# Score-tile windows, fewer matmuls on zeros, and another front in a planned attention and mixer kernel

## The chip, the core and the metric

The kernel runs on one core of a Trainium2 chip. The metric is the device time of one execution in microseconds (us); the kernel before takes 1763.97 us in the median of three runs (1763.39 to 1764.01). The engines are TensorE (PE in the profile, PEld for its weight loads), VectorE (DVE), ScalarE (ACT), GpSimd (POOL) and SyncE (SP), which issues nearly all of the transfers.

## What is computed

Two layers, each an attention block and a mixer over tokens, on x of 2048 tokens by 640 features. There are 32 heads of 20 features:

```python
def _A_ref(x, wqkv, wo):
    B, S, D = x.shape
    H = 32
    Dh = D // H
    qkv = (lambda x, *d: x.transpose(*d))((x @ wqkv).reshape(B, S, 3, H, Dh), 2, 0, 3, 1, 4)
    q, k, v = qkv[0], qkv[1], qkv[2]
    scores = jnp.einsum("bhqd,bhkd->bhqk", q, k) * (Dh ** -0.5)
    p = _softmax(scores, axis=-1)
    o = jnp.einsum("bhqk,bhkd->bhqd", p, v)
    return (lambda x, *d: x.transpose(*d))(o, 0, 2, 1, 3).reshape(B, S, D) @ wo

def _B_ref(x, w1, b1, w2, b2):
    h = _layernorm(x, axis=-1)
    u = jnp.einsum("bsd,sf->bdf", h, w1) + b1
    u = _gelu(u)
    y = jnp.einsum("bdf,fs->bds", u, w2) + b2
    return (lambda x, *d: x.transpose(*d))(y, 0, 2, 1)

x = x + _A_ref(_layernorm(x, axis=-1), A_wqkv, A_wo)
x = x + _B_ref(_layernorm(x, axis=-1), B_w1, B_b1, B_w2, B_b2)
```

The last two lines run twice. In each layer 32 x 2048 x 2048 scores have to be exponentiated, which is most of the work.

## The kernel before, in words

**Tiling.** Tokens are cut into 16 tiles of 128, queries into 4 blocks of 512, and heads into 8 groups of 4. A *unit* is one query block, one head group and one tile of keys (`unit_order`, line 468): four *chunks* of 128 keys by 512 queries, one for each head of the group. A chunk's scores are one matmul on a strip of 32 rows of the array (line 700), and the four heads' strips run beside each other. They land in a PSUM bank. There are eight banks: banks 0 to 2 form the wide score tile (three chunks), banks 3 and 4 the narrow one (two chunks), bank 6 accumulates the output, and banks 5 and 7 are shared by everything else.

**Two ways to exponentiate.** ScalarE takes the wide and the narrow tile in turn and applies Exp to three or two chunks at once (`do_exp`, line 880; the activation is line 887). VectorE takes whole units of its own, one bank per chunk: it scales each chunk to a 16-bit integer tile J (`do_J`, line 840), and then forms five terms T of J whose bit patterns, read as bf16, add up to the exponential (`do_T`, line 860). Which units go to VectorE is decided in `d_take` (line 786): a unit is taken if VectorE would end it before ScalarE gets to the end of that group.

**After the exponential** TensorE multiplies by V (`do_PV`, line 927), in groups of four chunks on four column strips. V is stored as `Vaug`, 24 columns for each head: 20 of values, one of ones, whose product is the softmax denominator, and padding. At a group's end VectorE transposes the sums (line 976) and takes a reciprocal (line 988), GpSimd multiplies (line 995), and VectorE transposes back (line 1003).

**Fills.** All other matrix work is cut into *fills* (`add_fill`, line 366): the projections of Q, K and V, the output projection, and the mixer's two products. A fill accumulates in bank 5 or 7 (in any free bank where no attention runs) and is copied out by ScalarE or VectorE (`copy`, lines 461 and 463; L456 and L453 are its matmuls). `do_fill` (line 410) runs a burst of up to 400 ns of one fill, and stops it early where the next matmul would end after `s_at[0] + FILL_OVER`, the time at which the next score tile can start; FILL_OVER is 0.0.

**What sets the order.** No scheduler reorders anything: under a manual schedule, `run_until` (line 1535) keeps one planned clock for each engine, asks each engine's chooser for its next job and start, and emits the earliest one. The planned durations are constants of the file. So the order on every engine is fixed when the program is built, and on the chip each engine runs its list in order and waits for semaphores. The planner for TensorE is `pe_choose`. It collects the options: the next score tile (priority 0), a score tile for VectorE (0.9), PV groups, and a fill (1 if urgent, else 4), each with its start. It then keeps those that start within 30 ns of the earliest, and those of priority 1 or better that start within a *window* of their own; the best priority wins:

```python
opts.append((s_at[0], 0, WIN_S[a.next_slot()], a.do_SA))
...
e0 = min(o[0] for o in opts)
ok = [o for o in opts if o[0] <= e0 + 30 or (o[1] <= 1 and o[0] <= e0 + o[2])]
o = min(ok, key=lambda o: (o[1], o[0]))
```

`WIN_S` (line 72) has that window for the wide tile (slot 0) and the narrow one (slot 1), in planned ns.

**Matmuls on zeros.** The same function keeps a history of TensorE's planned work in the last 3413 ns, counted in slots of 216 ns. Where the best option is more than 250 ns away and the history holds less than `HAM_MIN` (line 82), it emits a matmul on zeros instead (`do_warm`, line 1466). Ten more stand at the very start (line 1588).

**The front.** `front` (line 1556) loads four token tiles, the weights of Q and of K (`load_w`), two more token tiles, V's weights wv, and the other token tiles, all on SP's queue, which holds eight transfers at a time. The weights are copied into padded tiles by ScalarE or VectorE (`pad_copies`). Each token tile goes through statistics on VectorE (lines 343 to 346), a scale on GpSimd (`scale_job`, lines 354 and 356), its application on VectorE (line 530), transposes on TensorE (line 541) and a copy to hh. ScalarE zeroes the padding of Q's and K's weights (line 1586), and then writes V's padding and ones (lines 1591 and 1593). GpSimd follows with two small memsets of V (lines 1594 and 1596).

Of the kernel before, what the change touches and what calls it, by code (L numbers as in the profile page):

```python
# [21 lines left out]
H = 32  # L22
# [46 lines left out]
LAT_V = 120.0  # L69
EXP_CH = 453.0  # L70
D_SLACK = 0.0
WIN_S = (160.0, 160.0)
FILL_OVER = 0.0
M_F = 0.0
SD_WAIT = 500.0
# [3 lines left out]
FILL_NS = 400.0  # L79
COL_FILL = True  # L80
URG = 16
HAM_MIN = 10.0
DMA_RATE = 400.0
DMA_LAT = 1600.0

# [41 lines left out]
def kernel(  # L127
# [135 lines left out]
    def push(eng, prio, ready, dur, fn, ok=None, table=None):  # L263
        seq[0] += 1
        jobs[eng].append((prio, ready, seq[0], dur, fn, ok, table))
# [84 lines left out]
    def scale_job(prio, ready, mv, then, double):  # L350

        def f(start):
            rt = stat.tile([128, 1], F32, name="rt")
            nc.gpsimd.tensor_scalar(out=rt[:], in0=mv[:, 1:2], scalar1=(1.0 + LN_EPS) if double else 1.0,
                                    scalar2=LN_EPS * LN_EPS if double else LN_EPS, op0=ALU.mult, op1=ALU.add)
            nc.gpsimd.tensor_tensor(out=rt[:], in0=rt[:], in1=mhalf[:], op=ALU.pow)
            nmr = None
            if double:
                nmr = stat.tile([128, 1], F32, name="nmr")
                nc.gpsimd.tensor_tensor(out=nmr[:], in0=mv[:, 0:1], in1=rt[:], op=ALU.mult)  # L360
                nc.gpsimd.tensor_scalar(out=nmr[:], in0=nmr[:], scalar1=-1.0, scalar2=None, op0=ALU.mult)
            then(rt, nmr, start + (1250 if double else 900) + 150)
        push("POOL", prio, ready, 1250 if double else 900, f)


    def add_fill(mms, cost, evac, ecost, ready=0.0, pr=5, ok=None, urgent=None, acost=None, eprio=2, bf16=None, on_start=None,
# [1034 lines left out]
    def pe_choose():  # L1401
# [46 lines left out]
        o = min(ok, key=lambda o: (o[1], o[0]))  # L1448
        while hist and hist[0][0] < now - 3413:
            hist.popleft()  # L1450
        if o[0] > now + 250 and sum(h[1] for h in hist) < HAM_MIN and now > 2000:
            if a.want and not a.done and not a.acc_open():
                return (o[0], o[3])
            if a.want and not a.done or bank_free[5] is not None and bank_free[5] <= now:
                return (now + (SW if pe_mode[0] != "col" else 0.0), do_warm)
# [100 lines left out]
    def front(L0):  # L1556
        def load_x0(tt):
            def f(sl, t):
                tl = sb("x0", [128, D], BF16, sl)
                dma(tl[:], A_x[0, tt * 128:(tt + 1) * 128, :], 128 * D * 2, t,  # L1560
                    then=lambda t: L0.token_tile(tt, tl[:], t, lambda t: rX0.give(sl, t)))
            rX0.want(f)

        def load_w(i):
            wr = sb("wraw", [128, NDT, D], BF16, i)
            coff = 0 if i else D
            dma(wr[:], A_wqkv[:, coff:coff + D].rearrange("(dt p) n -> p dt n", p=128), 128 * NDT * D * 2,
                rate=DMA_RATE * (0.5 if i else 0.9), then=lambda t: pad_copies(i, wr, t))
        for tt in range(4):
            load_x0(tt)  # L1570
        load_w(1)
        load_w(0)
        for tt in range(4, 6):
            load_x0(tt)
# [12 lines left out]
        for _ in range(N_WARM0):  # L1587
            nc.tensor.matmul(ps(6, [128, 512])[0:32, :], lhsT=zw[:, 0:32], rhs=ident[:].unsqueeze(1).to_broadcast([128, 4, 128]), start=True, stop=True, tile_position=(0, 0))

        v_pad = Vv[:, :, :, DH:VW].rearrange("p k h c -> p (k h) c")  # L1590
        nc.scalar.activation(out=v_pad.bitcast(F32), in_=mhalf[:, 0:1].unsqueeze(2).to_broadcast([128, NKT * H, (VW - DH) // 2]),
                             func=ACT.Copy, scale=0.0)
        nc.scalar.activation(out=v_pad[:, :, 0:1], in_=mhalf[:, 0:1].unsqueeze(2).to_broadcast([128, NKT * H, 1]), func=ACT.Copy, scale=-2.0)
        nc.gpsimd.memset(Vaug[:, NKT * H * VW:], 0.0)

        nc.gpsimd.memset(Vv[:, :, H // 2, 0:32 - VW], 0.0)
        clk.update(ACT=6000.0, DVE=1100.0, POOL=2200.0, PE=1300.0 + 427.0 * N_WARM0)

    def late_weights():
        nc.gpsimd.memset(wo_pad[:].rearrange("p a b -> p (a b)"), 0.0)  # L1600
# [56 lines left out]
```

## Time and profile before

| | |
|---|---|
| Median of three runs | 1763.97 us |
| The profiled execution's own time | 1763.39 us |
| Its span, first to last instruction | 1761.6 us |
| PE, DVE, ACT, POOL busy | 1673.1, 1531.1, 1589.0, 181.1 us |
| Mean granted TensorE clock | 0.992 |
| Wide exponential (128x1536), 660 | 1486 ns each |
| Narrow exponential (128x1024), 659 | 1063 ns each |
| J, 796, and T, 995, on VectorE | 677 and 703 ns each |

In the profile a line such as `L887 ACT ACTIVATE P<-pst` is a group of instructions: source line, engine, operation, and what it writes and reads. After the bar come the busy time and the mean of one, and behind the next bar how long the engine had been idle ahead of them and what ended that. Durations of one instruction overlap a little with the next, so that a stream of exponentials starts them somewhat closer together than their mean. TensorE's busy time contains the matmuls on zeros. In the windows by stage each row has a stretch's start and end and its length, then the busy time of PE, PEld, DVE, ACT and POOL with the number of instructions, then the granted clock of TensorE as a share of full speed, the share of the transfer engines, and GB/s. The first layer's exponentials run from 20 to 817 us and the second layer's from about 870 to 1683 us; between 800 and 1000 us the first mixer's last products and the second layer's projections run too, and the second mixer's last products end the kernel.

### The profile page before, as it was taken

Reading aid. Unit: us, or ns where it says so; the run is one execution under the profiler, and the core shown is the slowest. Engines: PE = TensorE matmul, PEld = TensorE weight load, DVE = VectorE, ACT = ScalarE, POOL = GpSimd, SP = SyncE. Lnnn points to the kernel's source line nnn. Section 1 sums busy time; section 2 is a strip of 40 time slices with the busy share of each in tenths; the row PEclk is TensorE's granted clock in tenths of the full one; section 3 lists DMA queues with packets and bytes.
Section 4 is the critical chain, followed back from the end, with each engine's and each line's share of the span. In section 5 each row is a group of like instructions: output and inputs, shape, how many; then the busy total and the mean of one; then the engine's idle time right before and its main releaser. Section 6 shows DMA issues by size and latency. Waiting matters only on the chain.

```text
span 1761.6 us, 50941 instructions
## 1 busy us (share of the span) xinstructions
PE 1673.1 (95%) x22105; PEld 644.4 (37%) x22105; DVE 1531.1 (87%) x2715; ACT 1589.0 (90%) x1441; POOL 181.1 (10%) x297
## 2 busy tenths in 40 slices
PE   8999999999999999998999999999999999999989
PEld 3433233222333233334545432332333333333356
DVE  6788999999989999998444699999998999989973
ACT  7799999999999999997598799999999999999940
POOL 3100012000200020002100000210012000200010
PEclk8999999999999999999999999999999999999999
DMA  3200001000222015520422000100012210365133
GB/s 117 28 2 2 2 13 35 1 2 1 62 71 63 17 40 183 164 62 21 141 71 81 32 2 2 39 24 1 1 31 70 69 59 1 122 181 174 46 96 97
DMA packets 103298, 98.10 MB, mean 56 GB/s; under 512 B 45600, under 2 KB 79520, under 8 KB 103072
## 3 DMA queue, kind: packets, MB, share of 16 engines
q1 hardware_dynamic: 99456, 94.82, 17.6%
q8 instruction: 173, 2.83, 0.7%
q0 software_dynamic: 3616, 0.01, 0.3%
q14 instruction: 53, 0.43, 0.1%
HBM read 63.35 MB, written 31.46 MB: 54 GB/s over the span
## 4 chain that ended last, share of the span: by engine, by line
PE 45%; DVE 41%; ACT 7%; issue 4%; DMA 2%; POOL 1%; SPq 0%; DVEq 0%; POOLq 0%; ACTq 0%
DVE JT L860 17%; PE pst L456 15%; DVE JT L840 14%; PE pst L700 12%; PE pst L927 12%; ACT P L887 6%; PE pst L453 5%; DVE T_85 L976 2%; DVE attnT L1003 1%; DMA W<-in_B_w_dram 1%; DVE QT L463 1%; DVE x1last L1088 1%; DVE bnst L343 1%; DVE bnst L344 1%; DVE rden L988 1%
## 5 line engine op out<-in xcount | busy, mean ns | idle before, releaser
L887 ACT ACTIVATE P<-pst 128x1024 bf16<-128x1024 f32 (+1 forms) x1321 | 1512.5, 1273 | 42.8 <-PE pst L700 26.3
L860 DVE TENSOR_SCALAR JT<-JT 128x2048 uint16<-128x2048 uint16 x995 | 669.7, 703 | 3.2
L700 PE MATMUL pst<-QT,KT 32*128 32x512 bf16 (+1 forms) x4224 | 577.0, 377 | 33.9 <-ACT P L887 20.7
L840 DVE TENSOR_SCALAR JT<-pst 128x512 uint16<-128x512 f32 x796 | 528.0, 677 | 66.9 <-PE pst L700 47.7
L927 PE MATMUL pst<-P,Vaug 128*32 128x512 bf16 (+1 forms) x3396 | 516.3, 380 | 3.1 <-DVE T_85 L976 2.2
L927 PE MATMUL pst<-JT,Vaug 128*32 128x512 bf16 (+1 forms) x4140 | 499.9, 376 | 14.7 <-DVE T_85 L976 9.1
L700 PEld LDWEIGHTS <-KT 32*128 32x128 bf16 x4224 | 155.1, 91 | 501.4 <-issue 492.5
L927 PEld LDWEIGHTS <-Vaug 128*32 128x32 bf16 x7536 | 181.9, 94 | 319.3 <-issue 284.8
L995 POOL TENSOR_TENSOR T_86<-T_85,rden 128x512 bf16<-128x512 f32 x64 | 68.2, 1065 | 1184.4 <-DVE rden L988 1144.7
L1466 PE MATMUL pst<-ident,zw 128*32 128x512 bf16 (+1 forms) x390 | 125.7, 376 | 0.0
L456 PEld LDWEIGHTS <-W 128*32 128x32 bf16 x3384 | 88.7, 96 | 63.3 <-issue 31.5
L456 PE MATMUL pst<-wo,attnT 128*32 128x320 bf16 x1984 | 105.2, 301 | 3.7 <-DVE JT L840 1.4
L456 PE MATMUL pst<-hh,wq 128*32 128x512 bf16 x1232 | 102.9, 382 | 2.3 <-DVE JT L840 1.8
L456 PE MATMUL pst<-hh,wk 128*32 128x512 bf16 x1240 | 96.9, 381 | 1.5 <-DVE hh L463 0.7
L456 PE MATMUL pst<-x1last,W 128*32 128x320 bf16 x1536 | 81.6, 301 | 0.4
L456 PEld LDWEIGHTS <-attnT 128*32 128x32 bf16 x1984 | 49.6, 95 | 48.4 <-issue 32.4
L456 PE MATMUL pst<-attnT,hh 128*32 128x320 bf16 x1196 | 58.9, 300 | 3.2 <-ACT hh L461 0.7
L456 PE MATMUL pst<-JT,W 128*32 128x320 bf16 x1080 | 52.6, 300 | 0.3 <-issue 0.3
L1003 DVE STREAM_TRANSPOSE attnT<-T_86 128x512 bf16<-128x512 bf16 (+1 forms) x66 | 44.9, 682 | 2.1 <-POOL T_86 L995 2.0
L1466 PEld LDWEIGHTS <-zw 128*32 128x32 bf16 x390 | 35.2, 96 | 31.1 <-issue 17.3
L456 PE MATMUL pst<-hh,W 128*32 128x320 bf16 x768 | 40.5, 301 | 6.0 <-DMA W<-in_B_w_dram 4.7
L456 PEld LDWEIGHTS <-wq 128*32 128x32 bf16 x1232 | 32.6, 95 | 34.4 <-issue 20.2
(94 smaller groups left out, 893.4 us busy)
## 6 DMA issues: line engine op xcount, KB each, us to landing
W<-in_B_w_dram SPq DMA_DIRECT2D x10, 768.0 KB
W<-in_B_w_dram SPq DMA_DIRECT2D x24, 256.0 KB
xs<-in_A_x_dram SPq DMA_DIRECT2D x32, 160.0 KB
x2d<-xs SPq DMA_DIRECT2D x16, 320.0 KB
xs<-x2d SPq DMA_DIRECT2D x16, 320.0 KB
x1d_69<-xs SPq DMA_DIRECT2D x12, 320.0 KB
uacca_72<-W SPq DMA_DIRECT2D x12, 320.0 KB
W<-uacca_72 SPq DMA_DIRECT2D x12, 320.0 KB
```

The costliest lines, as they stand in the source:

```text
L343: nc.vector.bn_stats(out=bst[:, 0, :], in_=src[:, 0:half])
L453: nc.tensor.matmul(out_, lhsT=lhsT, rhs=rhs, start=start, stop=stop)
L456: nc.tensor.matmul(out_[32 * c:32 * c + 32], lhsT=lhsT[:, 32 * c:32 * c + 32], rhs=rhs, start=start, stop=stop, tile_position=(0, 32 * c))
L700: pe(nc.tensor.matmul(dst, lhsT=k_, rhs=q_, start=True, stop=True, tile_position=(32 * j, 0)))
L840: nc.vector.tensor_scalar(out=c["jt"][:, j * 512:(j + 1) * 512], in0=Dt[:], scalar1=SCALE * LOG2E * 256.0, scalar2=127.0 * 256.0, op0=ALU. ...
L860: nc.vector.tensor_scalar(out=tt_[:], in0=c["jt"][:], scalar1=0.5, scalar2=TERM_C[i], op0=ALU.mult, op1=ALU.add)
L887: nc.scalar.activation(out=P[:, 0:n, :].rearrange("p a b -> p (a b)"), in_=St[:, 0:n, :].rearrange("p a b -> p (a b)"), func=ACT.Exp, scal ...
L927: pe(nc.tensor.matmul(dst, lhsT=Vaug[:, n:n + 32], rhs=ap, start=acc["cnt"][j] == 1 and not part, stop=last[j] and (half is None or part = ...
L976: nc.vector.transpose(out=T1[:], in_=src[:, 0:w])
L995: eng.tensor_tensor(out=T2[:], in0=T1v, in1=rden.unsqueeze(2).to_broadcast([128, w // 32, 32]), op=ALU.mult)
L1003: nc.vector.transpose(out=attnT[(qb, g)][:, q0:q1], in_=T2[:].rearrange("p c i -> p (c i)"))
L1466: pe(nc.tensor.matmul(dst[0:32, 0:128 * n], lhsT=zw[:, 0:32], rhs=ident[:].unsqueeze(1).to_broadcast([128, n, 128]), start=not inside, sto ...
```

## The change

The window of the wide score tile goes from 160 to 330 ns, that of the narrow one from 160 to 100. The history below which a matmul on zeros is emitted goes from 10 to 8 slots, and none is emitted in the first 12 us of the plan (before: 2). The plan's durations for GpSimd's scale become shorter (1250 to 1000, and 900 to 750 ns), and so do its estimates of when the weights have landed. In the front, two token tiles are loaded ahead of Q's weights instead of four, and two between Q's and K's. V's padding and ones are written by four memsets on GpSimd, as a job of the plan with priority 5, not before 9 us and 4.6 us long, in place of ScalarE's two writes. FILL_OVER, and the place where a burst of fills stops, are the same in both files.

```diff
-WIN_S = (160.0, 160.0)
+WIN_S = (330.0, 100.0)
 FILL_OVER = 0.0
...
-HAM_MIN = 10.0
+HAM_MIN = 8.0
...
-            then(rt, nmr, start + (1250 if double else 900) + 150)
-        push("POOL", prio, ready, 1250 if double else 900, f)
+            then(rt, nmr, start + (1000 if double else 750) + 150)
+        push("POOL", prio, ready, 1000 if double else 750, f)
...
-        if o[0] > now + 250 and sum(h[1] for h in hist) < HAM_MIN and now > 2000:
+        if o[0] > now + 250 and sum(h[1] for h in hist) < HAM_MIN and now > 12000:
...
             dma(wr[:], A_wqkv[:, coff:coff + D].rearrange("(dt p) n -> p dt n", p=128), 128 * NDT * D * 2,
-                rate=DMA_RATE * (0.5 if i else 0.9), then=lambda t: pad_copies(i, wr, t))
-        for tt in range(4):
+                then=lambda t: pad_copies(i, wr, t))
+        for tt in range(2):
             load_x0(tt)
         load_w(1)
+        for tt in range(2, 4):
+            load_x0(tt)
         load_w(0)
         for tt in range(4, 6):
             load_x0(tt)
...
-        v_pad = Vv[:, :, :, DH:VW].rearrange("p k h c -> p (k h) c")
-        nc.scalar.activation(out=v_pad.bitcast(F32), in_=mhalf[:, 0:1].unsqueeze(2).to_broadcast([128, NKT * H, (VW - DH) // 2]),
-                             func=ACT.Copy, scale=0.0)
-        nc.scalar.activation(out=v_pad[:, :, 0:1], in_=mhalf[:, 0:1].unsqueeze(2).to_broadcast([128, NKT * H, 1]), func=ACT.Copy, scale=-2.0)
-        nc.gpsimd.memset(Vaug[:, NKT * H * VW:], 0.0)
-
-        nc.gpsimd.memset(Vv[:, :, H // 2, 0:32 - VW], 0.0)
-        clk.update(ACT=6000.0, DVE=1100.0, POOL=2200.0, PE=1300.0 + 427.0 * N_WARM0)
+        def v_ones(start):
+            nc.gpsimd.memset(Vv[:, :, :, DH:VW], 0.0)
+            nc.gpsimd.memset(Vaug[:, NKT * H * VW:], 0.0)
+            nc.gpsimd.memset(Vv[:, :, :, DH:DH + 1], 1.0)
+
+            nc.gpsimd.memset(Vv[:, :, H // 2, 0:32 - VW], 0.0)
+        push("POOL", 5, 9000.0, 4600.0, v_ones)
+        clk.update(ACT=5000.0, DVE=1100.0, POOL=2200.0, PE=1300.0 + 427.0 * N_WARM0)
```

## The prediction

> **What bounds the kernel now.** I read the page's busy times first, then the chain of waits, then the busy time by stage, then who waited for whom in the long attention stretches, and last the first 20 us on each engine.
>
> ```profile
> span 1761.6 us, 50941 instructions
> PE 1673.1 (95%) x22105; PEld 644.4 (37%) x22105; DVE 1531.1 (87%) x2715; ACT 1589.0 (90%) x1441; POOL 181.1 (10%) x297
> PE 45%; DVE 41%; ACT 7%; issue 4%; DMA 2%; POOL 1%; SPq 0%; DVEq 0%; POOLq 0%; ACTq 0%
> L887 ACT ACTIVATE P<-pst 128x1024 bf16<-128x1024 f32 (+1 forms) x1321 | 1512.5, 1273 | 42.8 <-PE pst L700 26.3
> L1466 PE MATMUL pst<-ident,zw 128*32 128x512 bf16 (+1 forms) x390 | 125.7, 376 | 0.0
> ```
>
> Three engines are close to full together. The second group is not work: 390 matmuls on zeros that only keep TensorE busy. By stage (PE, PEld, DVE, ACT, POOL busy, then granted clock):
>
> ```profile
> 100.00:800.00 700.00, 669.19 (x8724) 228.46 (x8716) 662.34 (x1134) 679.93 (x597) 64.10 (x90) 1.00 0.15 45
> 800.00:1000.00 200.00, 188.73 (x3016) 101.96 (x3013) 107.98 (x221) 152.38 (x162) 21.71 (x52) 0.99 0.24 76
> 1000.00:1600.00 600.00, 580.18 (x7651) 198.71 (x7650) 567.11 (x981) 583.29 (x512) 61.27 (x87) 1.00 0.16 49
> ```
>
> In the two attention stretches ScalarE is idle for only 20.1 of 700 us and 16.7 of 600 us, VectorE for 37.7 and 32.9. The chain passes often through VectorE, since what ends last alternates, but ScalarE has the least room. Of its idle time between 100 and 1600 us, and VectorE's, the largest parts that the attention loop makes are (us, times, longest):
>
> ```profile
> ACT P L887 <- PE pst L700: 24.4, 51, 2.2
> ACT P L887 <- PE pst L927: 8.7, 14, 1.7
> DVE JT L840 <- PE pst L700: 43.5, 79, 1.3
> ```
>
> So 24.4 us is all that a better-timed score tile could give back to the exponentials there. The clock matters next:
>
> ```profile
> 338.50:341.95 3.45, 2.08 (x25) 0.73 (x18) 3.34 (x6) 2.77 (x3) 0.00 (x0) 1.00 0.00 0
> 341.95:345.35 3.40, 3.28 (x18) 1.00 (x17) 3.37 (x8) 2.37 (x2) 1.05 (x1) 0.50 0.02 5
> 345.35:348.80 3.45, 3.45 (x41) 0.96 (x39) 3.15 (x6) 3.08 (x3) 0.00 (x0) 1.00 0.00 0
> ```
>
> TensorE was busy for 2.08 of 3.45 us (60%), with waits of 0.52, 0.62 and 0.35 us; then the clock was halved for 3.4 us. It happened once in the long attention stretches. Last, the front:
>
> ```profile
> 5.26 2.55 ACT L1593 ACTIVATE Vaug<-mhalf 128x512 bf16<-128x512 f32 x1
> 7.87 0.20 POOL L1596 MEMSET Vaug<- 128x128 bf16 x1 [5.69 <-ACT Vaug L1593]
> 8.16 0.19 POOL L354 TENSOR_SCALAR rt<-mv 128x1 f32<-128x1 f32 x1
> 9.53 0.71 PE L541 MATMUL pst<-ident,attnT 128*128 128x128 bf16 x5 [4.34 <-DVE attnT L530]
> GB/s 0 213 224 191 324 372 371 364 363 364 143 20 0 11 0 20 269 38 5 11 0 0 0 0 108 2 0 11 0 0 0 50 65 70 93 69 68 71 62 154
> ```
>
> GpSimd stood 5.7 us behind ScalarE's write of V's ones before it could scale the first token tile, whose statistics were ready at 4.2 us. The last line is the load rate in steps of 1.5 us.
>
> **The change part by part.** The kernel writes its instruction order at build time, so a constant moves every instruction; I compare the two built programs by counts. The words "fill bursts stop" have no edit behind them: that stop and its allowance (0.0) are in both, and runs of filling matmuls number 828 before and 832 after.
>
> *Front, taken −1 us.* Off ScalarE go two writes (1.09 + 2.55 = 3.64 us); they held the first scale from 4.2 to 8.16 us, so 3.9 us is the most to gain. What is late next: in the new order TensorE has eight of V's projections ahead of Q's, and they need wv, the ninth load, as before. Adding up the rate line, its 3.44 MB are in at about 13.0 us. The cold 512-column rows of wq took 3.15 us for 7 before, 0.43 each with the overlap off, so 320 columns take about 0.27 and eight of them 2.2 us; so Q starts at about 15.2 against 13.76 us before, though with more of V done; the ten cold projections follow, and the first exponential lands at 19.5 to 21, against 20.43. On SP, wq moves ahead of token tiles 2 and 3: those come 800 KB later, 2.2 us at 364 GB/s to 3.8 at 213, still before wv. On POOL four memsets (2048 + 512 + 136 elements) now stand ahead of tile 4's scale: by the row of wo's memset (5120 elements, 4.37 us) 2.3 us, or 4.6 by the plan; tile 4's scale ran only at 15.54. Should they hold VectorE's copies, the wait for wv covers about 2 us, and a longer one costs its excess. Ends −3.9 and +2.
>
> *ScalarE's work, taken +5.5.* The program after has 662 wide, 661 narrow and no single-bank exponentials, against 660, 659 and 2: 2 × 1.486 + 2 × 1.063 − 2 × 0.64 = +3.8 us (0.64 by the slope between the two). Its copies: K +4 × 0.592, Q +3 × 0.59, V −4 × 0.428, transposed tiles −1 × 0.693: +1.7. VectorE sheds 8 × 0.677 + 10 × 0.703 + about 3.5 of copies = 15.9 us. If ScalarE paces, +5.5; if VectorE did, its 41% of the chain would make −6.5. I take +5.5, since in both stretches ScalarE's busy share (97%) is above VectorE's (95%), so moved work lands on the fuller engine. Ends −6.5 and +5.5.
>
> *Zero matmuls, taken −1.5.* 400 become 161 (390 were profiled). They hold 10.2 us of the chain; in proportion the 239 gone are 6 us at most. But they sit in stretches without fills: 71 are between 1200 and 1300 us, where ScalarE is busy 99.2 and VectorE 98.7 of 100 us and nothing can be gained. Ends −6 and 0.
>
> *The clock, taken +5.6.* In that same stretch the zero matmuls are 22.9 of TensorE's 95.8 us, so without any it is 73% busy, and with half of them about 84%; at 60% the clock fell. The distance shrinks from 36 points to 24. I estimate four more drops in the roughly 440 us of such stretches, where there was one. Price: over the 10.3 us shown ScalarE was idle 2.08 us, 0.68 of it before the drop, so 1.4 us each. Ends 0 and 12 × 1.4 = 17.
> Here the Trainium skill speaks against my term: "TensorE: Matmul & The Clock Gate", section "Why this matters for your kernels", asks only that TensorE have no idle gap above about 3 us. The rows above show a drop after gaps of at most 0.62 us, so the measurement decides; by the page this term would be nothing and the sum 1764.4.
>
> *The windows for score tiles, taken −2.* A wide tile due within 330 ns (was 160) is now waited for, a narrow one within 100. In the built program the other TensorE work between a narrow tile and the next wide one falls from about 910 to 760 ns in stretches with fills (by the plan's 216 ns for a group of four), and between wide and narrow rises from 560 to 650. A wide tile has less time: it must come within the narrow exponential (1.063 us), the narrow one within the wide (1.486). So some of the 24.4 us goes; I take a sixth, −4. Queued behind TensorE's longer wait are VectorE's score tiles (43.5 us of waits) and the PV matmuls that give back P's buffers (8.7 us): I take +2. Ends −22 (nine tenths) and +8 (a sixth of those 52 us).
>
> Sum: −1 + 5.5 − 1.5 + 5.6 − 2 = +6.6 us. The profiled execution took 1763.39 us (span 1761.6 and 1.8 around it), 0.6 under the median of three. 1763.4 + 6.6 = 1770.0. The mid stage (800 to 1000) and the end keep their matmuls and cost nothing more: TensorE is 94% busy there with the same work.
>
> **The rivals.** *Faster: the wide tile's wait pays.* Place: the 24.4 us. If three quarters of it go (−18.3 in place of −4), the sum is 6.6 − 14.3, or 1755.7. The terms beside it are +10.6, so it decides from 14.1 us on (58% of the waits). For it: those waits are the attention loop's largest on ScalarE. Against: ScalarE runs at 97%, and in the waits of TensorE for ScalarE (17.5 us, 63 times) the tile is already ahead of time.
> *No difference.* Clock as before, extra ScalarE work covered by front and zero matmuls: −1 + 5.5 − 1.5 − 2 = +1, 1764.4. For it: the same matmuls, loads and exponentials but for 0.3%.
> *The clock collapses.* Twelve more drops: +17 instead of +5.6, 1781. For it: no zero matmul ran in the 338.5 to 342 stretch although its history was thin, since the plan did not foresee those waits; a lower threshold leaves less to lose. Against: one drop in 440 us so far.
>
> **How the numbers follow.** Forecast case 0.50, faster rival 0.24, no difference 0.16, collapse 0.10. A change under 0.2% (3.5 us) can't be told from none; faster 0.24, same 0.16, slower 0.60. The range leaves a tenth at each end: down past the faster rival's 1755.7 to 1755, up past the collapse's 1781 to 1785, for its unknown count.
>
> **What would show it.** Right: three to six half-clock stretches of 3.4 us inside 300–400, 700–800, 1200–1300 or 1400–1600 us; ScalarE's attention busy time up by about 5 us and VectorE's down by 16; waits of exponentials for L700 near 20 us; first exponential at 19.5 to 21 us; about 151 rows on zeros beside the opening ten. Wrong: those waits below 10 us with ScalarE at 98% or more (faster rival); no new clock drop (the +5.6 falls); a first exponential before 18 us (wv was not the cover); VectorE's waits for L700 above 60 us (the narrow side was undersized).

## The result, and the profile after

| | before | after |
|---|---|---|
| Median of three runs, us | 1763.97 (1763.39 to 1764.01) | 1777.54 (1775.09 to 1780.13) |
| Profiled execution, us | 1763.39 | 1775.09 |
| Its span, us | 1761.6 | 1773.3 |

The changed kernel is slower: ratio 1.0078, with a 95% interval of 1.0055 to 1.0101, or +13.6 us. The forecast was 1770.0, that is +6.0 on the median and +6.6 in its own sum. The sign and the range were right. The sum was about half of what came, and the experiments show that it was not put together from the right terms either.

From the page of the kernel after: the span, the busy time of the engines, the chain of waits by engine, and the groups of exponentials, score matmuls, VectorE's J and matmuls on zeros.

```profile
span 1773.3 us, 50343 instructions
PE 1644.9 (93%) x21810; PEld 648.3 (37%) x21810; DVE 1525.6 (86%) x2692; ACT 1585.8 (89%) x1446; POOL 189.6 (11%) x299
DVE 38%; PE 33%; ACT 19%; issue 9%; DMA 1%; POOL 0%; SPq 0%; DVEq 0%; POOLq 0%; ACTq 0%
L887 ACT ACTIVATE P<-pst 128x1536 bf16<-128x1536 f32 (+1 forms) x1323 | 1509.3, 1316 | 41.5 <-PE pst L927 21.4
L700 PE MATMUL pst<-QT,KT 32*128 32x512 bf16 (+1 forms) x4224 | 586.8, 377 | 69.6 <-ACT P L887 49.8
L840 DVE TENSOR_SCALAR JT<-pst 128x512 uint16<-128x512 f32 x788 | 524.3, 678 | 77.9 <-PE pst L700 61.4
L1466 PE MATMUL pst<-ident,zw 128*32 128x512 bf16 (+1 forms) x151 | 48.6, 365 | 0.0
```

Three things are to be seen. None of the three nearly full engines has more to do: ScalarE is busy 3.2 us less than before, VectorE 5.5 us and TensorE 28.2 us less, in a span that is 11.7 us longer. So the loss is idle time; ScalarE's total goes from 172.6 to 187.5 us. Second, in the exponentials' own row the idle time is nearly what it was (42.8 us before, 41.5 now), but what ended most of it has changed places: before it was the score tile (L700, 26.3 us), now it is the PV matmuls (L927, 21.4 us), which give back the buffer that an exponential writes. Third, TensorE now stands 49.8 us for exponentials (L887), where it stood 20.7 us before. In the chain of waits, where what ends last alternates, ScalarE's share rose from 7 to 19% and TensorE's fell from 45 to 33%. The row of the score matmuls before:

```profile
L700 PE MATMUL pst<-QT,KT 32*128 32x512 bf16 (+1 forms) x4224 | 577.0, 377 | 33.9 <-ACT P L887 20.7
```

The view of waits, 100 to 1600 us, after (us, times, longest):

```profile
DVE JT L840 <- PE pst L700: 58.6, 95, 2.1
PE pst L700 <- ACT P L887: 44.9, 138, 0.9
ACT P L887 <- PE pst L927: 18.7, 22, 3.3
ACT P L887 <- PE pst L700: 14.4, 32, 1.3
```

ScalarE's two waits were 24.4 and 8.7 us, which is 33.1 together. They are 14.4 and 18.7 now, which is 33.1 again. What the waits for score tiles (wide and narrow together) gave back, the waits for PV groups took. TensorE's longer wait for exponentials (44.9 us in this view, 17.5 before) isn't the reason. It is mostly where matmuls on zeros used to stand: in e6 (next section), which keeps the order of before and leaves out zeros, it is 40.6 us, and the wait for PV groups is 10.0; in e1, with the new windows and nearly all the zeros, it is 21.5, and the wait for PV groups 14.9. Why the PV groups come later is seen below for one place, and not shown for the rest. VectorE's waits for its score tiles rose from 43.5 to 58.6 us.

By stage (busy us of PE, PEld, DVE, ACT, POOL; then granted clock, transfer share, GB/s), after:

```profile
40.00:100.00 60.00, 52.90 (x810) 25.29 (x808) 46.08 (x78) 44.95 (x51) 9.26 (x6) 1.00 0.19 24
100.00:300.00 200.00, 190.25 (x2523) 66.97 (x2519) 171.44 (x288) 188.46 (x170) 20.42 (x28) 1.00 0.04 12
300.00:800.00 500.00, 463.36 (x6042) 162.25 (x6039) 476.01 (x826) 488.57 (x430) 45.89 (x61) 0.99 0.19 59
800.00:1000.00 200.00, 184.48 (x2884) 102.15 (x2884) 109.97 (x227) 148.68 (x153) 20.76 (x52) 0.97 0.24 76
1000.00:1600.00 600.00, 566.20 (x7572) 196.70 (x7561) 563.85 (x969) 582.13 (x517) 62.69 (x87) 1.00 0.14 42
```

and the first three of the same stretches before:

```profile
40.00:100.00 60.00, 55.46 (x859) 23.92 (x852) 46.47 (x81) 48.13 (x52) 9.14 (x6) 1.00 0.18 21
100.00:300.00 200.00, 194.97 (x2585) 65.00 (x2578) 182.48 (x306) 195.00 (x173) 21.51 (x29) 1.00 0.04 12
300.00:800.00 500.00, 474.22 (x6143) 163.46 (x6138) 479.85 (x829) 484.93 (x425) 42.58 (x61) 0.99 0.19 59
```

From 40 to 300 us ScalarE is idle 26.6 us where it was 16.9 (length less busy time, the two rows together). That is the stretch in which attention runs while Q, K and V are still being projected. From 300 to 800 us, the long steady stretch of the first layer, it is idle 11.4 where it was 15.1: there the change helps. This is the idle time of ScalarE by stage, worked out in the same way for the kernels that matter below (the experiments are described in the next section):

| us | before | after | e1: new windows alone | e9: new windows early only | e10: new windows late only |
|---|---|---|---|---|---|
| 0 to 40 | 8.6 | 12.0 | 8.4 | 8.3 | 9.0 |
| 40 to 100 | 11.9 | 15.1 | 17.5 | 17.4 | 11.9 |
| 100 to 300 | 5.0 | 11.5 | 6.7 | 8.3 | 3.3 |
| 300 to 800 | 15.1 | 11.4 | 12.2 | 10.9 | 6.5 |
| 800 to 1000 | 47.6 | 51.3 | 48.7 | 48.6 | 48.2 |
| 1000 to 1600 | 16.7 | 17.9 | 20.9 | 16.7 | 11.3 |
| sum | 104.9 | 119.2 | 114.3 | 110.2 | 90.3 |
| its difference to before | | +14.3 | +9.4 | +5.3 | −14.6 |
| span's difference to before | | +11.7 | +11.5 | +7.4 | −15.6 |

ScalarE's idle time thus follows the span within some 3 us in every column, so this table can be read as an account of where time is lost. One row needs care: in the kernel after, ScalarE no longer makes the two writes of V's padding and ones (1.09 and 2.55 us), so its additional 3.4 us in the first 40 are work that is gone and not time lost.

What the projections do between 40 and 100 us is seen in the waits of that stretch. After:

```profile
ACT KT L461 <- PE pst L456: 5.7, 4, 2.3
ACT Vaug L461 <- PE pst L456: 5.4, 4, 3.2
```

before:

```profile
ACT Vaug L461 <- PE pst L456: 4.1, 7, 1.1
ACT KT L461 <- PE pst L456: 1.5, 2, 0.9
```

ScalarE stands at the copies of K and V, 11.1 us in place of 5.6, because TensorE's fills (L456) end later. One cause is in TensorE's own timeline (start, length, what; in brackets the idle time and its releaser), after:

```profile
48.74 1.05 PE L456 MATMUL pst<-hh,wk 128*32 128x512 bf16 x16
52.54 0.40 PE L927 MATMUL pst<-JT,Vaug 128*32 128x512 bf16 x4 [2.75 <-DVE JT L860]
52.75 0.86 PE L456 MATMUL pst<-attnT,hh 128*32 128x320 bf16 x20
```

A PV group stands at the head of TensorE's list and waits 2.75 us for a term T that VectorE has not yet formed, and 20 matmuls of V's projections stand behind it, which start within 0.3 us of it. The list is fixed, so nothing can pass. Why the term is late is in the same view, in the rows of GpSimd and VectorE:

```profile
47.40 4.54 POOL L1602 MEMSET wo<- 128x5120 bf16 x1
48.35 4.13 DVE L860 TENSOR_SCALAR JT<-JT 128x2048 uint16<-128x2048 uint16 x1
```

A T takes 0.70 us in the mean. This one started beside GpSimd's memset of the padded output weights and took 4.13, until 0.5 us after the memset's end. Before the change the same memset ran too, but VectorE's list had other work beside it, which took its usual time, and the next T began after it:

```profile
41.71 4.37 POOL L1600 MEMSET wo<- 128x5120 bf16 x1
43.96 0.69 DVE L840 TENSOR_SCALAR JT<-pst 128x512 uint16<-128x512 f32 x1 [2.16 <-PE pst L700]
44.56 0.68 DVE L463 CAST KT<-pst 128x512 bf16<-128x512 f32 x1
```

So what the new order met here is an accident of where a T falls, as far as the trace shows. ScalarE's wait for V at this place, 3.24 us, is as large as all that it loses between 40 and 100 us (15.1 against 11.9). A second place where PV matmuls come late, in ScalarE's timeline at the end of the production:

```profile
276.32 4.89 ACT L887 ACTIVATE P<-pst 128x1536 bf16<-128x1536 f32 x4
284.50 2.37 ACT L887 ACTIVATE P<-pst 128x1536 bf16<-128x1536 f32 x2 [3.29 <-PE pst L927]
```

and TensorE's, which released it:

```profile
282.04 1.53 PE L456 MATMUL pst<-wo,attnT 128*32 128x320 bf16 x40
284.01 0.81 PE L927 MATMUL pst<-P,Vaug 128*32 128x512 bf16 x9 [0.43 <-DVE T_85 L976]
```

The PV matmuls of ScalarE's chunks waited for the accumulator, which VectorE had to transpose first (L976), after two terms of its own; TensorE ran the output projection meanwhile. Before the change no wait of an exponential for L927 shows between 100 and 300 us.

### The profile page after: what moved, and what is told of

It is laid out like the page before. It is cut to its first block, busy times and chain, and to the rows that moved or that the text cites. A ratio compares the mean times of both kernels' runs of the same rounds, so it can differ in the third digit from the quotient of the medians.

```text
span 1773.3 us, 50343 instructions
## 1 busy us (share of the span) xinstructions
PE 1644.9 (93%) x21810; PEld 648.3 (37%) x21810; DVE 1525.6 (86%) x2692; ACT 1585.8 (89%) x1446; POOL 189.6 (11%) x299
## 3 DMA queue, kind: packets, MB, share of 16 engines
q1 hardware_dynamic: 99456, 94.82, 17.4%
## 4 chain that ended last, share of the span: by engine, by line
DVE 38%; PE 33%; ACT 19%; issue 9%; DMA 1%; POOL 0%; SPq 0%; DVEq 0%; POOLq 0%; ACTq 0%
ACT P L887 19%; DVE JT L860 17%; DVE JT L840 13%; PE pst L456 10%; PE pst L700 9%; PE pst L927 8%; PE pst L453 5%; DVE T_85 L976 2%; DVE attnT L1003 1%; DVE QT L463 1%; DVE x1last L1088 1%; DVE xs L1078 1%; DVE rden L988 0%; DVE bnst L343 0%; DVE W L1231 0%
## 5 line engine op out<-in xcount | busy, mean ns | idle before, releaser
L887 ACT ACTIVATE P<-pst 128x1536 bf16<-128x1536 f32 (+1 forms) x1323 | 1509.3, 1316 | 41.5 <-PE pst L927 21.4
L700 PE MATMUL pst<-QT,KT 32*128 32x512 bf16 (+1 forms) x4224 | 586.8, 377 | 69.6 <-ACT P L887 49.8
L927 PE MATMUL pst<-P,Vaug 128*32 128x512 bf16 (+1 forms) x3404 | 511.4, 381 | 3.3 <-DVE T_85 L976 2.9
L927 PE MATMUL pst<-JT,Vaug 128*32 128x512 bf16 (+1 forms) x4100 | 490.3, 379 | 17.2 <-DVE JT L860 10.6
L700 PEld LDWEIGHTS <-KT 32*128 32x128 bf16 x4224 | 171.2, 91 | 518.6 <-issue 503.5
L927 PEld LDWEIGHTS <-Vaug 128*32 128x32 bf16 x7504 | 182.8, 95 | 329.9 <-issue 294.4
L456 PEld LDWEIGHTS <-W 128*32 128x32 bf16 x3384 | 91.2, 96 | 61.3 <-issue 37.5
L456 PE MATMUL pst<-wo,attnT 128*32 128x320 bf16 x1984 | 105.2, 301 | 5.9 <-DVE JT L840 2.7
L456 PE MATMUL pst<-hh,wq 128*32 128x512 bf16 x1240 | 104.9, 382 | 3.1 <-DVE JT L840 1.9
L456 PE MATMUL pst<-hh,wk 128*32 128x512 bf16 x1240 | 96.6, 381 | 3.4 <-ACT hh L461 1.6
L456 PE MATMUL pst<-x1last,W 128*32 128x320 bf16 x1536 | 80.7, 301 | 3.7 <-DVE W L1231 2.1
L456 PEld LDWEIGHTS <-attnT 128*32 128x32 bf16 x1984 | 50.1, 96 | 48.9 <-issue 34.0
L456 PE MATMUL pst<-attnT,hh 128*32 128x320 bf16 x1156 | 58.3, 305 | 1.1 <-ACT hh L461 0.5
L456 PE MATMUL pst<-JT,W 128*32 128x320 bf16 x1080 | 51.5, 300 | 0.1
L354 POOL TENSOR_SCALAR rt<-mv 128x1 f32<-128x1 f32 x64 | 13.8, 216 | 330.1 <-DVE mv L346 329.8
L1466 PE MATMUL pst<-ident,zw 128*32 128x512 bf16 (+1 forms) x151 | 48.6, 365 | 0.0
L1003 DVE STREAM_TRANSPOSE attnT<-T_86 128x512 bf16<-128x512 bf16 (+1 forms) x66 | 44.9, 682 | 3.5 <-POOL T_86 L995 3.4
L456 PEld LDWEIGHTS <-wq 128*32 128x32 bf16 x1240 | 32.0, 95 | 35.6 <-issue 22.6
L456 PEld LDWEIGHTS <-wk 128*32 128x32 bf16 x1240 | 32.2, 95 | 34.2 <-issue 20.2
```

What stands on the lines that cost most here:

```text
L456: nc.tensor.matmul(out_[32 * c:32 * c + 32], lhsT=lhsT[:, 32 * c:32 * c + 32], rhs=rhs, start=start, stop=stop, tile_position=(0, 32 * c))
L700: pe(nc.tensor.matmul(dst, lhsT=k_, rhs=q_, start=True, stop=True, tile_position=(32 * j, 0)))
L887: nc.scalar.activation(out=P[:, 0:n, :].rearrange("p a b -> p (a b)"), in_=St[:, 0:n, :].rearrange("p a b -> p (a b)"), func=ACT.Exp, scal ...
L927: pe(nc.tensor.matmul(dst, lhsT=Vaug[:, n:n + 32], rhs=ap, start=acc["cnt"][j] == 1 and not part, stop=last[j] and (half is None or part = ...
L1003: nc.vector.transpose(out=attnT[(qb, g)][:, q0:q1], in_=T2[:].rearrange("p c i -> p (c i)"))
L1466: pe(nc.tensor.matmul(dst[0:32, 0:128 * n], lhsT=zw[:, 0:32], rhs=ident[:].unsqueeze(1).to_broadcast([128, n, 128]), start=not inside, sto ...
```

## The experiments

All ratios are against the kernel before, run on the same chip at the same time, with 95% intervals; its medians were 1765.72 (e1, e2, e3, e6), 1763.71 (e9 to e12) and 1764.2 us (e5, e8, e13, e14), and its single runs lay between 1758.6 and 1770.5 us. So ratios are what is compared, not single times. Conversions to us multiply the ratio's distance from 1 by that median. The shorter plan times of GpSimd's scale were not run by themselves.

**e1, the windows alone.**

```diff
-WIN_S = (160.0, 160.0)
+WIN_S = (330.0, 100.0)
```

> The kernel before with the windows of the score tiles alone at 330 and 100 ns; front and matmuls on zeros as before. Theory F (the front is what costs: in the changed kernel the groups' results are 5.6 us late at 147 us, 13.7 us late at 288 us and 13.0 us late at 1690 us) expects 1762 to 1767 us. Theory W (the longer wait costs: TensorE's waits for ScalarE rose from 20.7 to 49.8 us and VectorE's for score tiles from 47.7 to 61.4) expects 1770 to 1777.

Measured: 1773.33 us, ratio 1.0051 [1.0031, 1.0072], or +9.0 us. The windows alone lose two thirds of what the whole change loses, as the theory of the longer wait (W) expected. The mean clock is 0.994 against 0.992 before, so half clock is not what it is lost to. In the page, idle time ahead of the exponentials is 41.5 us, 21.9 of it ended by the score tile.

**e2, the rule for zeros alone.**

```diff
-HAM_MIN = 10.0
+HAM_MIN = 8.0
...
-        if o[0] > now + 250 and sum(h[1] for h in hist) < HAM_MIN and now > 2000:
+        if o[0] > now + 250 and sum(h[1] for h in hist) < HAM_MIN and now > 12000:
```

> The kernel before with the thinner history alone (8 slots, none in the first 12 us); windows and front as before. Theory C (fewer matmuls on zeros let the clock fall: 7 half-clock stretches after the front in the changed kernel's trace against 5) expects 1768 to 1772 with more half-clock stretches than before. Theories F and W expect 1762 to 1766.

Measured: 1761.72 us, 0.9974 [0.9960, 0.9987], or −4.6 us, slightly better than either theory expected, though in its profiled execution TensorE's clock was halved for 45.0 us in nine stretches (before: 27.3 us in five). The order changes with the rule, so this run holds a new plan as well as fewer zeros.

**e6, fewer zeros in the order of before.** To part these two, the plan is kept, and of the matmuls that it places on zeros only two in five are emitted (156 of 390).

```diff
-        pe(nc.tensor.matmul(dst[0:32, 0:128 * n], lhsT=zw[:, 0:32], ...
+        if n_warm[0] % 5 in (0, 2):
+            pe(nc.tensor.matmul(dst[0:32, 0:128 * n], lhsT=zw[:, 0:32], ...
```

> The kernel before in exactly its own order, but of its 390 planned matmuls on zeros only two in five are emitted (156), as many as the changed kernel has. No instruction else moves. Theory C (clock) expects 1767 to 1772 with three or more new half-clock stretches inside attention. Theory F expects 1761 to 1765, since a matmul on zeros neither helps nor hinders there. Faster than 1761 would mean that the zeros themselves stood in the way.

Measured: 1765.06 us, 1.0001 [0.9988, 1.0014]. Its profiled execution has ten half-clock stretches, 45.2 us in all; over all runs the mean clock is 0.988, where the runs of before beside it have 0.991 (some 11 us more of half clock). Fewer zeros and more half clock together cost no time that can be told. Windows of this kernel about one of the stretches:

```profile
795.00:798.40 3.40, 1.81 (x29) 0.80 (x31) 3.37 (x7) 3.40 (x4) 0.00 (x0) 0.99 0.00 0
798.40:801.80 3.40, 3.40 (x44) 1.17 (x39) 3.40 (x6) 2.91 (x3) 1.05 (x1) 0.50 0.00 0
```

TensorE was busy 1.81 of 3.40 us, then its clock was 0.50. In the halved stretch ScalarE was idle 0.49 us, and VectorE not at all. This one isn't new: before has a drop at 795.9 us, after 3.42 us in which TensorE was busy for 1.83. More drops did come in e6, as the prediction's clock term said. What they cost by themselves the run can't tell, since it also removes the zeros, and the two could cancel. The runs of the unchanged kernel say something on it: of the 61 beside the experiments, the 19 with a mean clock of 0.990 or less took 1768.0 us on average and the 21 with 0.993 or more 1762.2. A straight line through all 61 gives 0.29 us of time for each us of half clock (95%: 0.23 to 0.35), about 1.0 us for a drop of 3.4. That is a correlation, and what halves the clock may also cost time in another way. The Trainium skill, "TensorE: Matmul & The Clock Gate", section "🎯 Why this matters for your kernels", asks for no idle gap above about 3 us between bursts. The longest wait ahead of this drop was 1.00 us, so that rule doesn't foretell these drops.

**e3, the front alone**: the new order of loads, the plan's rates of the weights, V's memsets on GpSimd, and ScalarE's plan starting at 5 us; without the shorter plan times of the scales.

```diff
-        for tt in range(4):
+        for tt in range(2):
             load_x0(tt)
         load_w(1)
+        for tt in range(2, 4):
+            load_x0(tt)
         load_w(0)
...
+        push("POOL", 5, 9000.0, 4600.0, v_ones)
```

> The kernel before with the new front alone (two token tiles ahead of Q's weights, the load estimates, V's ones and padding by four memsets on GpSimd). Theory F expects 1771 to 1778, with the first exponential near 22 us. Theories W and C expect 1763 to 1766, with the delay of the first exponential (1.6 us) at most.

Measured: 1769.91 us, 1.0025 [1.0009, 1.0040], or +4.4 us, between the ranges of the theories. The first exponential comes at 20.46 us, against 20.43 before, so this loss isn't a late first exponential.

**e14, V's memsets alone** (GpSimd instead of ScalarE, ScalarE's plan starting at 5 us; the load order of before):

```diff
-        nc.scalar.activation(out=v_pad.bitcast(F32), in_=mhalf[:, 0:1]...
-        nc.scalar.activation(out=v_pad[:, :, 0:1], in_=mhalf[:, 0:1]...
+        def v_ones(start):
+            nc.gpsimd.memset(Vv[:, :, :, DH:VW], 0.0)
+            nc.gpsimd.memset(Vaug[:, NKT * H * VW:], 0.0)
+            nc.gpsimd.memset(Vv[:, :, :, DH:DH + 1], 1.0)
...
+        push("POOL", 5, 9000.0, 4600.0, v_ones)
```

> The kernel before with only V's ones and padding by memsets on GpSimd; loads and their order as before. The whole new front gave +4.4 us. If the memsets are what costs, +2 to +5 us with VectorE's copies beside them stretched; if the order of the loads is, within 2 us of before, or a little faster, since GpSimd's first scale no longer stands behind ScalarE's writes.

Measured: 1765.04 us, 0.9995 [0.9976, 1.0014]. The first exponential comes at 18.75 us, 1.7 us earlier than before, since the first scale no longer stands behind ScalarE's write; the total doesn't move. Set beside e3, the cost of the front lies in what e3 has more, the load order with its planned rates, or in the plan that follows from them. That is by difference between two groups of runs; the load order was not run by itself.

**e5, the changed kernel with the front of before.**

```diff
-        for tt in range(2):
+        for tt in range(4):
             load_x0(tt)
         load_w(1)
-        for tt in range(2, 4):
-            load_x0(tt)
...
-        push("POOL", 5, 9000.0, 4600.0, v_ones)
-        clk.update(ACT=5000.0, DVE=1100.0, POOL=2200.0, PE=1300.0 + 427.0 * N_WARM0)
+        clk.update(ACT=6000.0, DVE=1100.0, POOL=2200.0, PE=1300.0 + 427.0 * N_WARM0)
```

> The changed kernel with the front of before (loads, load estimates, V's ones by ScalarE). If the parts add up (windows +8.9, thinner history -4.6, front +4.4 us), 1766 to 1772 us. If the loss of the first 150 us belongs to the windows (they alone were 6.7 us behind there, the changed kernel 5.6), the front adds nothing to it and the time stays within 3 us of the changed kernel's 1777.5.

Measured: 1775.63 us, 1.0063 [1.0042, 1.0083], against 1.0078 [1.0055, 1.0101] of the whole change. The first exponential is back at 20.09 us, from 22.01, and ScalarE is idle 8.4 us in the first 40 instead of 12.0 (its two writes are back); but 16.7 us instead of 15.1 from 40 to 100. On top of the windows and the new rule for zeros the front costs nothing that these runs can tell.

**e8, the changed kernel with V's padding and ones written early by ScalarE.** Only who writes them is changed:

```diff
+        nc.scalar.activation(out=v_pad.bitcast(F32), in_=mhalf[:, 0:1]...
+        nc.scalar.activation(out=v_pad[:, :, 0:1], in_=mhalf[:, 0:1]...
...
-            nc.gpsimd.memset(Vv[:, :, :, DH:VW], 0.0)
-            nc.gpsimd.memset(Vv[:, :, :, DH:DH + 1], 1.0)
```

> The changed kernel in its own order, but V's zeros and ones are written by ScalarE ahead of the loads as before; GpSimd keeps the two small memsets. In the changed kernel the GpSimd memsets ran from 12.2 to 16.7 us, and beside them VectorE's scaling of the fourth token tile took 1.71 us (0.45 alone) and its copy of wk 2.76 us (0.32 alone). If GpSimd's memsets hold up VectorE and with it the first projections, both fall to under 0.6 us, the first exponential comes 1 to 2.5 us ahead of 22.01, and the time falls by 1 to 4 us. If the late weights of V set that time, nothing moves.

Measured: 1777.70 us, 1.0080 [1.0054, 1.0105]. This run explains the late first exponential of the changed kernel, and shows that it doesn't matter. Timelines of GpSimd, VectorE and TensorE after:

```profile
12.24 1.80 POOL L1593 MEMSET Vaug<- 128x2048 bf16 x1
14.10 2.52 POOL L1595 MEMSET Vaug<- 128x512 bf16 x1
12.51 1.71 DVE L530 TENSOR_SCALAR attnT<-xs,mv,rt 128x640 bf16<-128x640 bf16 x1
14.14 2.76 DVE L463 COPY wk<-JT 128x640 bf16<-128x640 bf16 x1
14.28 0.71 PE L541 MATMUL pst<-ident,attnT 128*128 128x128 bf16 x5 [1.68 <-DVE attnT L530]
14.78 2.34 PE L453 MATMUL pst<-attnT,hh 128*128 128x320 bf16 x8
```

and of e8, VectorE and TensorE:

```profile
11.31 0.44 DVE L530 TENSOR_SCALAR attnT<-xs,mv,rt 128x640 bf16<-128x640 bf16 x1
11.67 0.32 DVE L463 COPY wk<-JT 128x640 bf16<-128x640 bf16 x1
13.15 2.29 PE L453 MATMUL pst<-attnT,hh 128*128 128x320 bf16 x8 [0.63 <-DMA attnT<-in_A_wqkv_dram]
```

The same two instructions of VectorE take 0.44 and 0.32 us alone, and 1.71 and 2.76 us beside the memsets; each then ends within 0.3 us of the end of the memset that it ran beside (14.04 and 16.62). V's eight projections, which stand behind the token tile's transposes in TensorE's list, start at 14.78 in place of 13.15 us, and the first exponential at 22.01 in place of 20.34. In e8 V's projections wait for wv, as the prediction had it, and wv is there at 13.15. The Trainium skill, "SBUF — State Buffer", section "🔬 SBUF: two separate sides", says of the port pair that VectorE and GpSimd share that it is "an **exclusive lock**, not a bandwidth split", held for the whole instruction; these rows agree. The total is the same with and without (1.0080 and 1.0078), though a gain of 1 to 4 us had been expected.

**e9 and e10, the windows in parts.** A layer has 512 units. In e9 the new windows hold for the first 96 of them, in which the projections run beside attention, and the old ones after; in e10 it is the other way round. Everything else is as before.

```diff
-WIN_S = (160.0, 160.0)
+WIN_S = (330.0, 100.0)
+WIN_L = (160.0, 160.0)
...
-                opts.append((s_at[0], 0, WIN_S[a.next_slot()], a.do_SA))
+                opts.append((s_at[0], 0, (WIN_S if a.now_unit() < 96 else WIN_L)[a.next_slot()], a.do_SA))
```

(e10 has the same line, with the two pairs of constants exchanged.)

> The kernel before with windows of 330 and 100 ns only until the first 96 of a layer's 512 units are taken, and 160 and 160 from there on. The run with the windows everywhere was 9.7 us behind at its third pair of groups (185 us) and gained little more in that layer. Theory P (the longer wait costs while a layer's projections are still being made: TensorE idles, and keys and V come late) expects nearly all of that run's loss, 1770 to 1776 us. Theory S (it costs in the steady stretches, through VectorE's score tiles) expects 1763 to 1768.

> The reverse: windows of 160 and 160 ns for the first 96 units of each layer, 330 and 100 after that. Theory P expects 1761 to 1767 us. Theory S expects 1770 to 1775.

Measured: e9 1772.94 us, 1.0049 [1.0030, 1.0069], or +8.6 us; e10 1749.12 us, 0.9915 [0.9897, 0.9933], or −15.0 us. The new windows in the production stage alone cost as much as everywhere; in the rest alone they make the kernel faster than both given versions, and faster than either theory expected. Waits of e10, 100 to 1600 us (its lines have numbers higher by one):

```profile
DVE JT L841 <- PE pst L701: 53.0, 83, 1.5
PE pst L701 <- ACT P L888: 21.6, 68, 0.6
ACT P L888 <- PE pst L928: 10.4, 21, 1.1
ACT P L888 <- PE pst L701: 8.5, 20, 1.4
```

Here the wait for score tiles falls from 24.4 to 8.5 us and the PV groups' rises only from 8.7 to 10.4: 18.9 in all where before and after have 33.1. VectorE's waits rise by 9.5 us and cost nothing that is seen. The stages of e10 show the gain where its windows hold, and ScalarE above 98% there:

```profile
300.00:800.00 500.00, 475.51 (x6271) 166.89 (x6267) 477.36 (x833) 493.48 (x435) 45.42 (x62) 1.00 0.19 59
1000.00:1600.00 600.00, 576.57 (x7560) 197.69 (x7559) 565.26 (x977) 588.67 (x518) 58.71 (x86) 1.00 0.15 45
```

and e9 the loss where its windows hold (the clock was halved for a part of this stretch, which it wasn't in the changed kernel, whose row above has 1.00 and ScalarE idle for 15.1 us, where e9 has 17.4 and before 11.9):

```profile
40.00:100.00 60.00, 53.22 (x780) 24.92 (x778) 43.15 (x73) 42.56 (x48) 9.27 (x6) 0.94 0.18 24
```

Before, e9, e10 and e1 are the four corners of one square, old or new windows early, old or new late: 0, +8.6, −15.0, +9.0 us. If the parts added up, e1 would be −6.4. It is 15 us slower than that. So the late windows are worth 15.0 us behind the early plan of before, and nothing that can be told behind the new early plan. The stage table says where: behind the new early plan, from 1000 to 1600 us ScalarE is idle 16.7 us with old late windows (e9) and 20.9 with the new (e1); behind the old one 16.7 and 11.3.

**e11 and e12, other windows.** Is it this pair of constants, or any new plan? e11 takes the wide side alone, e12 moves it by only 20 ns.

```diff
-WIN_S = (160.0, 160.0)
+WIN_S = (330.0, 160.0)
```

and for e12

```diff
-WIN_S = (160.0, 160.0)
+WIN_S = (180.0, 160.0)
```

> The kernel before with the wide tile's window at 330 ns and the narrow one's left at 160. If the longer wait for the wide tile is the cause, 1770 us or more; if the shorter window of the narrow tile is, 1763 to 1767.

> The wide tile's window at 180 instead of 160 ns, all else as before: too small an edit to mean anything by itself, but every instruction's place is planned anew. It shows how far a new plan alone scatters: under 3 us either way, if a single part's result is to be read as that part's; 5 us or more would mean that no part below that size can be.

Measured: e11 1765.50 us, 1.0009 [0.9996, 1.0021]; e12 1766.48 us, 1.0008 [0.9995, 1.0021]. Neither can be told from no change in total. By the rule set beforehand for e12, under 3 us either way, a single part's result can then be read as that part's; and by the one for e11, the narrow tile's window would be the cause. But within the run both moved. By the sums used in the table above, ScalarE's idle time from 40 to 300 us is 23.3 us in e11 and 22.7 in e12, where before has 16.9; from 300 to 800 us it is 6.5 and 9.0, where before has 15.1. So each of the three other settings that were tried in the production stage loses 6 to 9 us of ScalarE's time there against the plan of before, even the one that differs by 20 ns. The early loss is therefore not a property of 330 and 100, nor of the narrow window. A part of it goes with what was seen above: in all seven kernels with other windows in that stage (after, e1, e5, e8, e9, e11, e12) a T of VectorE falls beside the memset of the output weights and takes 4.13 us or more, TensorE then stands 2.5 to 3.5 us for it, and ScalarE is idle 15.0 to 17.5 us from 40 to 100 us; in the other seven (before, e2, e3, e6, e10, e13, e14) no T does, and it is idle 11.9 to 13.0. By this reading 160 and 160 were lucky for this part. No run moved the memset, so it isn't shown by an experiment, and the rest of the loss, 100 to 300 us, is not explained by it. In e11 and e12 the steady stretch makes the loss up; in e1 and e9 it does so only in part.

**e13, the best version with the new rule for zeros** (e10 and the edit of e2 together).

> The kernel before with windows of 330 and 100 ns from unit 96 of each layer on, and the thinner history (8 slots, none in the first 12 us). Apart they gave -14.6 and -4.6 us. If they add up, 1743 to 1747 us; if both live on the same waits of ScalarE for score tiles (24.4 us in before, 8.5 with the late windows), 1747 to 1751.

Measured: 1753.92 us, 0.9938 [0.9914, 0.9963], where e10 had 0.9915 and e2 0.9974. Two edits that each gain give together no more than the first alone, and rather less: it came out above both ranges that had been expected.

## Why the prediction was right or wrong

What was right is the sign, with "slower" as the likeliest, and the engine to watch: ScalarE's idle time accounts for the loss. That the sum came out positive was luck: without the clock's +5.6 and the moved work's +5.5 it would have been −4.5, and neither of the two is found in the result as it was worked out. Its steps, one by one, with the measured time of each part alone:

| step | predicted, us | measured, us |
|---|---|---|
| windows and moved work | −2 + 5.5 = +3.5 | e1: +9.0 (+5.5 to +12.7) |
| fewer zeros and the clock, same order | −1.5 + 5.6 = +4.1 | e6: +0.2 (−2.1 to +2.5) |
| the same with its own plan | | e2: −4.6 (−7.1 to −2.3) |
| front | −1 | e3: +4.4 (+1.6 to +7.1); on top of the rest: not told from nothing |
| sum | +6.6 | e1 + e2 + e3: +8.8; the whole change: +13.6 |

*Windows, −2: the step that failed most.* It priced the windows by the waits of 100 to 1600 us, took a sixth of 24.4 us as gain and +2 for what is queued behind TensorE. The gain was larger (10.0 us of that wait went, to 14.4, where about 20 had been said), and the +2 was far too small: the PV groups' wait took those 10.0 us back, and VectorE's waits for its tiles rose by 15.1. (The upper end of +8 was to be a sixth of 52 us, which is 8.7.) The prediction named beforehand what would prove the step wrong on the narrow side, VectorE's waits above 60 us: they are 58.6 after, just under it, and 63.5 in e1. And the stretch from 40 to 100 us was not priced at all, where TensorE's list holds the projections that ScalarE and VectorE need and where a T now falls beside GpSimd's memset; a third of ScalarE's additional idle time from 40 to 300 us (3.2 of 9.7 us) arose there. The stretch from 800 to 1000 us, put at nothing, holds another 3.7 us of ScalarE's idle time.

*The faster rival.* Its mechanism exists. It asked for more than 14.1 of the 24.4 us, and for waits below 10 us with ScalarE at 98%; e10 has 8.5 us and 98.7 and 98.1% in the two steady stretches (493.48 of 500, 588.67 of 600), and is 15 us faster. In the change as given 10.0 us went, under that point, and were given back.

*The clock, +5.6.* Three to six drops were expected in certain stretches; after has two there (at 757.5 and 781.4 us, in 700 to 800). Before has two there as well, at 341.95 us, which the prediction shows, and at 795.9, which it missed when it counted one. So none of the four more came where they were expected. The whole profiled execution has eight half-clock stretches, 37.5 us, against five of 27.3; the new ones lie between 800 and 1000 and after 1650 us. The price of 1.4 us for a drop is of the order of the 1.0 that the runs of before suggest, but for fewer zeros and more half clock together e6 has nothing. Where the collapse rival had twelve more drops, there are three more stretches.

*Zeros, −1.5.* About 151 rows were predicted, and 151 came. Alone, without the clock's term, this can't be measured, since the one brings the other.

*ScalarE's work, +5.5.* The built program does have four more wide and narrow exponentials and two single ones less, but ScalarE's busy time in L887 fell from 1512.5 to 1509.3 us instead of rising by 5, while the mean record grew (1273 to 1316 ns). Records of neighbours overlap: those after add up to 1741.1 us (1011.0 wide, 730.1 narrow) in 1509.3 us of busy time. So adding up means of records, as the step did, isn't ScalarE's time. VectorE shed 5.5 us in place of 16. The term can't be found in the result.

*Front, −1.* The order of events was right: V's projections wait for wv, which was there at 13.15 us (e8), worked out as about 13.0. The first exponential was said to come at 19.5 to 21 and came at 22.01. The failed part is the memsets: 2.3 us by the nearest row was taken beside the plan's 4.6, and they lasted from 12.24 to 16.72, 4.5 us; the excess over the cover of wv was 1.6 us (14.78 against 13.15), which the prediction had allowed for as an end. But e8 takes that away and changes nothing, and e14 brings the first exponential to 18.75 and changes nothing: in none of these pairs does the time of the first exponential carry through to the end.

*The sum.* The deeper fault is the form: a sum of terms, each against the plan of before, though the prediction itself says that a constant moves every instruction. The square of e9, e10 and e1 misses additivity by 15 us, which is more than the whole effect, and e13 misses it again. What is shown is that interaction. What stays open is why the late windows gain nothing behind the early plan that they make themselves: the stage table places it (300 to 800 and 1000 to 1600 us), but no run takes apart which waits of those plans are to blame. Open too is what the shorter plan times of the scales do, which no run has alone. How much of e10's 15 us belongs to the windows, and how much to a plan that happens to fit, is open as well; e11 and e12, with 6.5 and 9.0 us of idle time from 300 to 800, speak for the first in that stretch, and with 18.0 and 19.1 us from 1000 to 1600 they don't in the other.

## What to carry to other kernels

Where a planner fixes the order at build time, its constants should be priced and tried by stage: the same window cost 9 us in the stage that still produces its inputs, a part of it by an accident of order, and gained 15 us behind it, and the best of these kernels (e10, 1749.12 us, ratio 0.9915) is neither of the two given. A sum of separately priced edits isn't to be trusted in such a kernel; a square of four runs tells quickly whether two edits add up. Where the engine that waits is TensorE, look at what stands behind the wait in its list, and count the waits of one consumer together (33.1 us before, 33.1 after), not only the one that was to be shortened.

## What the runs showed of the hardware that was not expected

- TensorE's clock was halved after stretches of 3.4 us in which it was 60% (before, 341.95 us) and 53% busy (e6, 798.4 us), with no wait above 1.00 us. Runs of the unchanged kernel with more half clock were longer, by 0.29 us for each us of it; leaving out three zeros in five in the same order (e6) gave more half clock and no longer time, 1.0001 [0.9988, 1.0014].
- GpSimd's memset of 512 single bf16 elements per partition, 24 elements apart, took 2.52 us (4.9 ns each); that of 2048 in runs of four took 1.80 us (0.9 ns each). A quarter of the elements, at as many places, took longer.
- These memsets read nothing from SBUF, and still a copy of VectorE that takes 0.32 us by itself took 2.76 us beside them, in e14 three copies of wq took 2.43 us (0.78 before), and a T took 4.13 us beside the memset of wo (0.70 in the mean). VectorE's J beside that memset, which reads PSUM, took its usual 0.69 us.
